# A channel-mixing MLP and an S4D convolution on one core: the 64-row remainder of layer 1 as three matmuls in two row halves of the array

## The chip, the core and the metric

The kernel runs on one core of a Trainium2 chip. The metric is device time in microseconds (us) of one execution; the time before is 1094.99 us, the median of three runs (1094.75 to 1095.13). Six names recur. PE is TensorE (its weight loads are listed as PEld), DVE is VectorE, ACT is ScalarE, POOL is GpSimd, and SP is the engine that issues most of the DMA transfers. PSUM is the memory into which PE writes, in banks of 512 float32 per partition.

## The reference

For 2048 tokens of 576 channels the kernel computes a normalisation, two branches from it, and their gated product with a skip connection:

```python
xn = _layernorm(x)
s = _A_ref(xn, ...)              # S4D: a convolution over all 2048 tokens, one kernel K per channel,
                                 #   K = 2 Re sum_n C[d,n] exp(A[d,n] dt[d] l), plus u * D_skip
g = _silu(_B_ref(xn, ...))       # MLP: layernorm -> 576x4608 (+b1) -> gelu -> 4608x576 (+b2)
return x + s * g
```

All values are float32, so the kernel has to keep more digits than one reduced-precision pass of PE gives.

## The kernel before

**The MLP** is most of PE's work. Its operands are split into a high part (rounded to float32r, a reduced form of float32) and a low part (what the rounding lost), and three products are summed in PSUM: high by high, high by low, low by high. The 4608 hidden features are cut into 12 groups of three tiles of 128 (`G = 3`), and the 2048 tokens into four blocks of 512. A *slot* is one group with one block: 48 slots, numbered from 0. Two blocks share a sweep over all groups, so the slots run in two sweeps of 24. A slot has eleven *positions*: three of layer 1 (one for each hidden tile, `layer1`) and eight of layer 2 (`layer2`, 72 matmuls of 288 columns).

**Layer 1** of a tile multiplies 576 input channels, which are four blocks of 128 rows and a remainder of 64. The four blocks take 12 matmuls with 512 columns (`w1h` with `XH`, `w1h` with `XL`, `w1l` with `XH`). The remainder takes two more. `XR` holds its 64 high rows above its 64 low rows, `w1r` holds the high weights twice, and `w1s` (called `r2` in the code) holds the low weights twice; `w1r` by `XR` and `w1s` by `XR` are full matmuls of 128 rows. So a tile has 14 matmuls, of which the last is needed for 64 rows only.

**The 64-row form.** `pair` (L608) computes that last product another way, ahead of the tile: with 64 rows of weights, in one half of the array's rows. For tile 0 it uses the upper half with `XR[:64]`, for tile 2 the lower half with a copy of the same rows in partitions 64 to 127 (`XQ`, loaded by `load_pair`, L604; it borrows the memory of `bias2` and is called `bias` in the profile). The two write two halves of one PSUM tile (`Q1[0]`), and `BEGUN` tells `layer1` to leave out the full matmul and not to clear PSUM. Tile 1 keeps its full one. The copy is loaded in 42 of the 48 slots, during the slot before; not where `bias2` is in use.

**The S4D branch** is computed as short *visits* of PE between the MLP's matmuls: `kgen` (L1042 in the profile) makes the convolution's kernel; `x1` (L1157), `k1` (L1188) and `s2` (L1217) are forward transform steps, `inv` (L1260) and `i1` (L1286) inverse ones. All of them split the array into smaller tiles of rows and columns; `x1` alone uses the shape that `pair` uses, 64 rows by 128 columns. DVE and ACT work between the visits.

**The order** of all engines' work is written out when the program is built. The class `Order` keeps a clock for each engine, charges each step an estimated duration, and puts steps into the program in that order. Dense work (layers 1 and 2) goes through `unit`; after a position `pe_turns` looks through lines of waiting steps (`c1`, `c3`, `kl` for S4D) and inserts visits whose inputs should be there, subject to spacing rules (`END`, `EDGE`, `ALONE`, `DUE`). With `edge`, at the end of a slot, it puts `pair` ahead of the visit, if the weights and the copy should have arrived; without a visit there, the slot has no pair. `hold` and the table `HOLD` delay single steps by hand. The names `mxa` and `mxb` are two PSUM tiles of two banks each that slots take in turn (`mx`); `cv` names those of the visits.

Of the kernel before, what the change touches and what calls it, by code (L numbers as in the profile page):

```python
# [18 lines left out]
P = 128  # L19
# [13 lines left out]
G = 3  # L33
NG = F // (P * G)
KB = 4
TB = 512
# [15 lines left out]
class Order:  # L52
# [44 lines left out]
    def take(self, eng, dur, ready, tbl=None):  # L97
        start = max(self.t[eng], ready)
        if eng == "DVE" and self.shared and start < self.t["POOL"] - 0.4:
            dur *= 1.1  # L100
        if tbl and tbl != self.tbl:
            dur += 1.28
            self.tbl = tbl
        self.t[eng] = start + dur
        return start + dur + self.LAT
# [119 lines left out]
def mixer_kernel(ctx, tc, u, log_a_real, a_imag, c_real, c_imag, log_dt, d_skip, w1, b1, w2, b2,  # L225
                 f1, f2, g2, g1, tvals, ident, out, parts=("mlp", "s4d")):
    nc = tc.nc
# [6 lines left out]
    def bank2(name):  # L234
        return ps.tile([P, 2, TB], F32, name=name, bufs=2 if name == "cv" else 1)
# [134 lines left out]
    acc = sb.tile([P, 8, D], F32, name="acc")  # L370
# [30 lines left out]
    MV, SECOND, PAIR, M4, SINGLE = {}, [], {}, [], {}  # L401
# [70 lines left out]
    XR = sb.tile([P, 2, TB], F32R, name="XR")  # L472
    XQ = {}
# [58 lines left out]
    W = {}  # L532
# [56 lines left out]
    HID, LAST, Q1, Q2, IDM = {}, {}, {}, {}, []  # L589
    turn = [0]  # L590

    def mx(i):
        return "mxa" if (turn[0] + i) % 2 == 0 else "mxb"

    BEGUN = set()
# [10 lines left out]
            XQ[0] = sb.tile([P, D], F32R, name="bias2")[:, :TB]  # L606
        nc.sync.dma_start(XQ[0][64:].bitcast(F32), XR[:64, tb].bitcast(F32))

    def pair(tb):

        Q1[0] = bank2(mx(1))
        for e, x in enumerate((XR[:64, tb], XQ[0][64:])):
            r, k = slice(64 * e, 64 * e + 64), e * (G - 1)
            nc.tensor.matmul(Q1[0][:, e], W[1][3][r, k * P:(k + 1) * P], x, start=True, stop=False,  # L616
                             skip_group_check=True)
        BEGUN.update((0, G - 1))

    def layer1(g, tb, i):  # L620
        h, lo, r1, r2 = W[1]
        c = slice(i * P, (i + 1) * P)
        if i < 2 and i not in BEGUN:
            Q1[i] = bank2(mx(i))
        q = Q1[i % 2][:, i // 2]
        ops = []
        for a, b in ((h, XH), (h, XL), (lo, XH)):
            ops += [(a[:, kb, c], b[:, kb, tb]) for kb in range(KB)]
        ops.append((r1[:, c], XR[:, tb]))
        if i not in BEGUN:  # L630
            ops.append((r2[:, c], XR[:, tb]))
        for j, (a, b) in enumerate(ops):
            nc.tensor.matmul(q, a, b, start=j == 0 and i not in BEGUN, stop=j == len(ops) - 1, skip_group_check=True)  # L633
        return hidden(g, tb, i, q)

    def first_layer1(i):


        h, lo, r1, r2 = W[1]
        if i != 1:  # L640
            Q1[i] = bank2("mxb" if i else "mxa")
        q = Q1[2][:, 0] if i == 2 else Q1[0][:, i]
        pairs = [(h, XH, 0), (h, XH, 1), (h, XL, 0), (h, XH, 2), (h, XL, 1), (h, XH, 3), (h, XL, 2), (h, XL, 3)]

        if i != 1:
            for j, (a, b, kb) in enumerate(pairs):
                for k in ((0, 1), (2,))[i // 2]:
                    nc.tensor.matmul(Q1[k // 2 * 2][:, k % 2], a[:, kb, k * P:(k + 1) * P], b[:, kb, 0],  # L648
                                     start=j == 0, stop=False)
        c = slice(i * P, (i + 1) * P)  # L650
        for kb in range(KB):
            nc.tensor.matmul(q, lo[:, kb, c], XH[:, kb, 0], start=False, stop=False)
        for r in (r1, r2):
            nc.tensor.matmul(q, r[:, c], XR[:, 0], start=False, stop=r is r2)

        return [hidden(0, 0, k, Q1[k // 2 * 2][:, k % 2]) for k in ((), (0, 1), (2,))[i]]
# [296 lines left out]
    def tables(b):  # L953
# [37 lines left out]
        def weigh(part):  # L991
# [10 lines left out]
            else:  # L1002
# [7 lines left out]
                 step("DVE", dve(SB * NV), f(phase, 0), need=[("kg", b - 2)] if b > 1 else []),  # L1010
                 step("DVE", dve(n), f(phase, 1), hold=HOLD.get(("phase", b), 0)), step("ACT", act(SB * NV), whole),
                 step("DVE", dve(SB * NV), frac, hold=HOLD.get(("frac", b), 0)), step("ACT", act(SB * NV), fold, mark=("fold", b))],
                [step("ACT", act(SB * NV), f(sin, 0), need=[("fold", b)], mark=("sin", b, 0), tbl="sin"),
# [55 lines left out]
        return behind  # L1069


    X1, S2, INV, I1, KG = 1.5, 1.75, 2.15, 3.05, 1.03

    HOLD = {("weigh", 19, 3): 1, ("phase", 19): 1, ("frac", 18): 2, ("k", 2, 1): (2, 1), (2, 0, 24): 1, (2, 1, 24): 1, ("k1", 2, 1, 2): 1}

    def chunk(c):

# [240 lines left out]
    NPOS = G + 8  # L1318
    NSLOT = 4 * NG
    od = Order(tc, nc)  # L1320
    od.pinned = True
    el, wl2, wl, nl2, pl, pl2, nl, ml, ml2, xl, wx, c3, c2, c1, c4, kl, tl, sl, vl, gl, odl, fl = [od.line() for _ in range(22)]
    nlh, mlh, mlt = od.line(), od.line(), od.line()
    od.lines = od.lines[-3:] + od.lines[:-3]

# [76 lines left out]


    L1 = 14 * 0.2315
    LEN = [L1] * G + [3 * n * 0.132 + 0.02 for n in (4, 2, 2, 4, 3, 3, 3, 3)]

    T0 = 12.5
    for e, t in dict(PE=0.0, ACT=4.6, DVE=3.7, POOL=3.8, SP=0.0).items():
# [71 lines left out]
    def weigh_in(which):  # L1480

        m = KB + 1 if which == 1 else G
        end = od.t["PE"] + sum(LEN[G:] if which == 1 else LEN[:G])
        for i in range(m):
# [22 lines left out]
    def wmark(n, which):  # L1507

        per = KB + 1 + G
        a = n * per + (0 if which == 1 else KB + 1)  # L1510
        return [("w", k) for k in range(a, a + (KB + 1 if which == 1 else G))]
# [23 lines left out]
    for k in range(8):  # L1535
        gl["steps"].append(step("POOL", 0.7, lambda k=k: part.update({k: load_f2(k)}), mark=("f2", k),
                                need=[("f2c", k - 2)] if k > 1 else ["turns"]))
        fl["steps"].append(step(None, 4.5, lambda: None, need=[("f2", k)]))
        for f in range(2):
            fl["steps"].append(step("ACT", act(256), lambda k=k, f=f: part[k](f), mark=("f2c", k) if f else None,  # L1540
                                    need=[("f2s", k - 1)] if k and k % 2 == 0 else []))
# [33 lines left out]


    pace = dict(left=NCH * (2 + 2 + 4), last=0.0, started=False)
    END = 1000.0


    EDGE = 0.2, 0.6
    ALONE, DUE = 20.0, (160.0, 950.0)

    def pe_turns(limit=1, any_time=False, all_lines=True, edge=None):
        for x in (nl, pl, ml) + ((c3, c1, kl) if all_lines else ()):
            n = 0
            while n < (2 if x in (c1, nl) else limit):
                h = od.head(x)
                if h is None or h[0]["eng"] != "PE" or h[1] > od.t["PE"] + (0.3 if x is nl else -0.4):
                    break  # L1590
                if x is c1:
                    now = od.t["PE"]
                    gap = (END - now) / max(pace["left"], 1)
                    if n == 0 and pace["started"] and now < pace["last"] + EDGE[edge is None] * gap and not any_time:
                        break
                    pace["started"], pace["last"] = True, now
                    pace["left"] -= 1
                if x is kl and pace["started"]:
                    b = kl["steps"][0]["mark"][1]
                    wait = ("wu", b + 1) not in od.marks or od.t["PE"] < DUE[0] + b * (DUE[1] - DUE[0]) / NB  # L1600
                    if b < NB - 1 and od.t["PE"] < h[1] + (ALONE if wait else 3.0):
                        break
                if edge is not None and not BEGUN and x in (c3, c1, kl):
                    m = wmark(edge // 2, 1) + [("xq", edge)]
                    if all(k in od.marks and od.marks[k] < od.t["PE"] - 0.3 for k in m):
                        od.unit(lambda: pair(edge % 2), 0.24)
                behind = ride(h[0]) if x in (c1, c3) else None
                od.run(x)
                if behind:
                    behind()  # L1610
                od.pin()
                od.advance(od.t["PE"])
                n += 1

    LATER = {}

    def later(slot, pos, f):
# [22 lines left out]

        return od.t["PE"] + sum(LEN[k % NPOS] for k in range(pos + 1, q))

    GAP = 0.17

    def hidden_by(pos, i, o=0):
        n = when(pos, o + (G if i < G - 1 else G + 2))
# [24 lines left out]
    for slot in range(NSLOT):  # L1671
        turn[0] = slot + 1
        od.shared = slot > 1
        g, tb = slot // 2 % NG, slot % 2
        n = slot // 2
        final = slot >= NSLOT - 2
        for pos in range(NPOS):
            if pos < G:
                need = wmark(n, 1) + [("x", tb)]
                if pos == 0:  # L1680
                    od.force(lambda: all(m in od.marks for m in need))

                    if slot in (1, 2 * NG + 1):
                        od.marks["x", tb] -= 2.3
                cell = []
                od.unit(lambda: cell.extend([layer1(g, tb, pos)] if slot else first_layer1(pos)),
                        L1 * (14 - (pos in BEGUN)) / 14 if slot else L1 * (22, 6, 14)[pos] / 14, need)
                if pos == 2:
                    BEGUN.clear()
                    k = slot % (2 * NG)  # L1690
# [16 lines left out]
            else:  # L1707
                j, terms, last, hid = l2_terms(pos - G)
                need = [wmark(n, 2)[i] for i in hid] + [("h", slot, i) for i in hid]
# [6 lines left out]
                cell = []  # L1716
# [3 lines left out]
                b = 8 + 4 * tb + j  # L1720
                if halves:
                    dh = terms[0][1]
                    od.marks["z", dh] = od.t["PE"] + od.LAT
                    x = od.line()
# [3 lines left out]
                if split:  # L1728
                    add = cell[0]
                    for d in range(2) if j == 0 else (terms[0][1],):  # L1730
                        m = ("acc", slot, j, d)
# [3 lines left out]
                        x = od.line()  # L1735
# [3 lines left out]
                if last and not halves:  # L1739
# [4 lines left out]
                    elif final:  # L1744
                        x = el if slot < NSLOT - 1 else od.line()
# [12 lines left out]
            for f in LATER.get((slot, pos), ()):  # L1758
                f()
            od.advance(od.t["PE"])  # L1760
            pe_turns(edge=slot + 1 if pos == NPOS - 1 else None, all_lines=pos in (0, 1, 2, G + 1, G + 3, G + 5, NPOS - 1))
    od.force(lambda: not od.urgent and not any(x["steps"] for x in od.lines))


# [52 lines left out]
```

## Time and profile before

| What | Value |
|---|---|
| Median of three runs | 1094.99 us (1094.75 to 1095.13) |
| The profiled execution, its own time | 1095.67 us |
| Its span, first to last instruction | 1093.9 us |
| Granted TensorE clock, mean | 0.999 |
| PE busy, DVE busy, ACT busy | 99%, 82%, 66% of the span |
| Matmuls of 64 rows by `pair`, L616 | 32, in 16 slots |
| Loads of the copy, `bias<-XR` | 42 |

In rows of the profile a group reads: line, engine, operation, what is written and read, shape, and how often; then busy time and mean duration. A row of the timeline reads: start in us, length in us, engine, line, operation, names, shape of the array's tile (rows\*columns), operand, and how many instructions follow each other under that name. A matmul's length is its latency; successive matmuls overlap, so what one costs PE is the distance to the next start. The visits' float32 matmuls are run as two instructions each, so `kgen` has 64 in the profile and 32 in the program's order.

### The profile page before, as it was taken

How to read it: one execution, taken by the hardware profiler on the slowest of the kernel's cores; microseconds unless marked ns; L12 is line 12 of the kernel's file. 1: busy time of each engine (PE TensorE's matmuls, PEld its weight loads, DVE VectorE, ACT ScalarE, POOL GpSimd, SP SyncE). 2: the span in 40 equal slices, each digit the busy share in tenths (PEclk: the TensorE clock that was granted, in tenths of full speed). 3: DMA queues.
4: the chain of work that ended last, by engine and by line, in shares of the span. 5: the costliest groups of instructions: out<-in, count | busy, mean ns of one | idle time of the engine just before them, and what ended most of it. 6: DMA issues, size and time to landing. Idle time of an engine off the chain costs nothing.

```text
span 1093.9 us, 27052 instructions
## 1 busy us (share of the span) xinstructions
PE 1087.1 (99%) x11445; PEld 954.0 (87%) x11445; DVE 891.9 (82%) x1302; ACT 727.1 (66%) x1113; POOL 188.4 (17%) x261
## 2 busy tenths in 40 slices
PE   9999999999999999999999999999999999999998
PEld 7989899899888898888988888888888888888897
DVE  7798667889998879889899987997969888766367
ACT  6585699778676674767767848685675757534333
POOL 4566210153020100001100000000001021101132
PEclk9999999999999999999999999999999999999999
DMA  8746764626354152355624215143142434454444
GB/s 242 225 149 152 236 235 143 179 80 157 116 160 134 44 112 67 96 110 148 161 48 118 78 56 141 34 122 87 56 126 42 144 101 132 114 170 150 137 151 103
DMA packets 139553, 138.22 MB, mean 126 GB/s; under 512 B 88952, under 2 KB 105016, under 8 KB 138856
## 3 DMA queue, kind: packets, MB, share of 16 engines
q1 hardware_dynamic: 124424, 85.05, 29.0%
q0 software_dynamic: 14528, 50.71, 14.7%
q8 instruction: 89, 1.46, 0.6%
q10 hardware_dynamic: 480, 0.74, 0.3%
q14 instruction: 32, 0.26, 0.1%
HBM read 102.17 MB, written 36.63 MB: 127 GB/s over the span
## 4 chain that ended last, share of the span: by engine, by line
PE 95%; DVE 3%; ACT 1%; SPq 1%; issue 0%; DMA 0%; POOL 0%; DVEq 0%; ACTq 0%; POOLq 0%
PE mxb L707 20%; PE mxa L707 20%; PE mxa L633 20%; PE mxb L633 20%; PE cv L1217 3%; PE cv L1042 3%; PE cv L1260 2%; PE cv L1286 2%; PE cv L1188 1%; PE cv L1157 1%; PE mxa L1348 1%; DVE acc L717 0%; PE mxa L648 0%; SPq L1089 0%; PE mxb L616 0%
## 5 line engine op out<-in xcount | busy, mean ns | idle before, releaser
L677 DVE TENSOR_TENSOR hl<-h,hh 128x512 fp32r<-128x512 f32 x144 | 98.5, 687 | 99.2 <-ACT hh L674 98.4
L707 PE MATMUL mxa<-w2h,hh 128*128 128x288 f32 x573 | 170.3, 297 | 0.0
L707 PE MATMUL mxb<-w2h,hh 128*128 128x288 f32 x573 | 170.2, 297 | 0.0
L707 PE MATMUL mxb<-w2h,hl 128*128 128x288 f32 x573 | 169.3, 295 | 0.1
L707 PE MATMUL mxa<-w2h,hl 128*128 128x288 f32 x573 | 169.1, 295 | 0.0
L707 PE MATMUL mxa<-w2l,hh 128*128 128x288 f32 x573 | 168.6, 294 | 0.0
L707 PE MATMUL mxb<-w2l,hh 128*128 128x288 f32 x573 | 168.6, 294 | 0.0
L671 ACT ACTIVATE h<-mxa,b1t 128x512 f32<-128x512 f32 x73 | 50.1, 687 | 98.3 <-PE mxa L633 95.1
L707 PEld LDWEIGHTS mxa<-w2h,hh 128*128 128x128 f32 x573 | 107.6, 188 | 5.8 <-issue 3.0
L707 PEld LDWEIGHTS mxb<-w2h,hh 128*128 128x128 f32 x573 | 107.6, 188 | 4.3 <-issue 1.4
L707 PEld LDWEIGHTS mxb<-w2l,hh 128*128 128x128 f32 x573 | 107.6, 188 | 0.8
L707 PEld LDWEIGHTS mxa<-w2l,hh 128*128 128x128 f32 x573 | 107.6, 188 | 0.6
L707 PEld LDWEIGHTS mxb<-w2h,hl 128*128 128x128 f32 x573 | 107.5, 188 | 0.3 <-DVE hl L677 0.3
L707 PEld LDWEIGHTS mxa<-w2h,hl 128*128 128x128 f32 x573 | 107.5, 188 | 0.0
L671 ACT ACTIVATE h<-mxb,b1t 128x512 f32<-128x512 f32 x71 | 48.8, 687 | 69.7 <-PE mxb L633 67.2
L674 ACT ACTIVATE hh<-h 128x512 fp32r<-128x512 f32 x144 | 90.7, 631 | 3.7
L944 POOL DMA_DIRECT2D par<-par_s x36 | 27.8, 771 | 367.8 <-DVE mg L988 325.0
L717 DVE TENSOR_TENSOR acc<-mxa,acc 128x576 f32<-128x576 f32 x87 | 65.5, 753 | 26.0 <-PE mxa L707 25.9
L717 DVE TENSOR_TENSOR acc<-mxb,acc 128x576 f32<-128x576 f32 (+1 forms) x89 | 65.9, 741 | 17.8 <-PE mxb L707 17.7
L633 PE MATMUL mxa<-XH,w1h 128*128 128x512 f32 x284 | 79.2, 401 | 0.0
L633 PE MATMUL mxb<-XH,w1h 128*128 128x512 f32 x280 | 77.7, 399 | 0.0
L633 PE MATMUL mxa<-XL,w1h 128*128 128x512 f32 x284 | 76.1, 390 | 0.0
(277 smaller groups left out, 2494.4 us busy)
## 6 DMA issues: line engine op xcount, KB each, us to landing
raw<-in_B_w_dram SPq DMA_DIRECT2D x72, 288.0 KB, 3.4
raw<-in_B_w_dram SPq DMA_DIRECT2D x96, 192.0 KB, 3.5
par_s<-A POOLq DMA_DIRECT2D x4, 2160.0 KB, 8.1
par<-par_s POOLq DMA_DIRECT2D x36, 240.0 KB, 3.6
f2t<-f2q SPq DMA_DIRECT2D x24, 256.0 KB, 3.6
g2t<-g2p SPq DMA_DIRECT2D x24, 256.0 KB, 4.1
bias<-XR SPq DMA_DIRECT2D x42, 128.0 KB, 3.6
raw<-in_B_w_dram SPq DMA_DIRECT2D x48, 96.0 KB, 3.7
```

Of the source, the lines that this page charges most:

```text
L633: nc.tensor.matmul(q, a, b, start=j == 0 and i not in BEGUN, stop=j == len(ops) - 1, skip_group_check=True)
L671: nc.scalar.activation(t, q, AF.Gelu_apprx_tanh, bias=b1t[:, k:k + 1], scale=1.0)
L674: LAST[0] = nc.scalar.activation(hh[:, i], t, AF.Copy)
L677: nc.vector.tensor_sub(hl[:, i], t, hh[:, i].bitcast(F32))
L707: nc.tensor.matmul(q[:, dh, :288], a[:, i, c], b[:, i, d], start=i == 0 and k == 0 and alone != 1, stop=i == G - 1 and k == 2, skip_group_ ...
L717: nc.vector.tensor_add(o, q[:, dh:dh + n, :288], b)
L944: nc.gpsimd.dma_start(PAR[b].rearrange("p (g i) k -> p g (i k)", g=4), dram(par_s, (b // 3 * 48 + b % 3 * 4) * NPAR, [[D * NPAR, P], [12 * ...
L1042: nc.tensor.matmul(q[32 * g:32 * g + 32, i // 2, i % 2 * 64:i % 2 * 64 + 64], U[:, ri, 4 * g + i, :], v[:, ri, 4 * g + i, :], start=ri == ...
L1157: nc.tensor.matmul(Q[24 * v][:, e], FP[0][r, f, 0], x[r, 12 * e:12 * e + 12], start=n == 0, stop=n == 2, skip_group_check=True)
L1217: nc.tensor.matmul(Q[i][32 * q:32 * q + 32, f, ri::2], m[r, 4 * i + q, 32 * ri:32 * ri + 32], A2[r, 4 * p + 2 * i + q // 2, :, :, q % 2], ...
L1260: nc.tensor.matmul(QI[q // 2][64 * f:64 * f + 64, q % 2, i], MAT["g2t", p + i // 2][r, i % 2, f, ri], YS[p + i // 2][0][r, i % 2, ri, f], ...
L1286: nc.tensor.matmul(Q[h][64 * y:64 * y + 64, t], g1t.rearrange("p a e -> p (a e)"), A2[:, k:k + 2, 1].rearrange("p i d r -> p i r d"), star ...
```

## The change

`pair` now issues three matmuls, for all tiles of a slot: tile 0 in the upper row half, tile 2 in the lower, tile 1 in the upper half again, into a second PSUM tile (`Q1[1]`). They come at one of two places. At the edge of a slot they stand *behind* the visits, if there were any, and if the addition of the slot before that reads the second PSUM tile should be done. Otherwise they stand *within* layer 1, after tile 0 (`late`), behind visits that are put there or, where there are none, by themselves; tile 0's sum then ends with them. Numbers of the planner change too: charged durations of the visits, `END`, `EDGE`, `ALONE`, `DUE`, the order of two lines, and the table `HOLD` is emptied. Layer 2, the visits' own matmuls and all loads are as before.

```diff
-    def pair(tb):
-        Q1[0] = bank2(mx(1))
-        for e, x in enumerate((XR[:64, tb], XQ[0][64:])):
-            r, k = slice(64 * e, 64 * e + 64), e * (G - 1)
-            nc.tensor.matmul(Q1[0][:, e], W[1][3][r, k * P:(k + 1) * P], x, start=True, stop=False,
-                             skip_group_check=True)
-        BEGUN.update((0, G - 1))
+    def pair(tb, late):
+        r2, x = W[1][3], (XR[:64, tb], XQ[0][64:])
+        def mm(e, q, i, a, n, start=True, stop=False):
+            nc.tensor.matmul(q[:, a:a + n], r2[64 * e:64 * e + 64, i * P:(i + 1) * P], x[e][:, a:a + n], start=start,
+                             stop=stop, skip_group_check=True)
+        if not late:
+            Q1[0] = bank2(mx(1))
+        Q1[1] = bank2(mx(1 if late else 2))
+        mm(0, Q1[0][:, 0], 0, 0, TB, not late, late)
+        mm(1, Q1[0][:, 1], 2, 0, TB)
+        mm(0, Q1[1][:, 0], 1, 0, TB)
+        BEGUN.update(range(G))
...
-    X1, S2, INV, I1, KG = 1.5, 1.75, 2.15, 3.05, 1.03
-    HOLD = {("weigh", 19, 3): 1, ("phase", 19): 1, ("frac", 18): 2, ("k", 2, 1): (2, 1), (2, 0, 24): 1, (2, 1, 24): 1, ("k1", 2, 1, 2): 1}
+    X1, S2, INV, I1, KG = 1.38, 1.69, 1.99, 3.19, 1.03
+    HOLD = {}
...
-    END = 1000.0
-    EDGE = 0.2, 0.6
-    ALONE, DUE = 20.0, (160.0, 950.0)
+    END = 974.0
+    EDGE = 0.34, 0.29
+    ALONE, DUE = 18.4, (108.0, 794.0)
+    PAIR = 0.62, 0.53
...
-                if edge is not None and not BEGUN and x in (c3, c1, kl):
-                    m = wmark(edge // 2, 1) + [("xq", edge)]
-                    if all(k in od.marks and od.marks[k] < od.t["PE"] - 0.3 for k in m):
-                        od.unit(lambda: pair(edge % 2), 0.24)
+                away += x in (c3, c1, kl)
...
+        if away and edge is not None and not BEGUN:
+            m = wmark(edge // 2, 1) + [("xq", edge), ("acc", edge - 1, 3)]
+            if all(k in od.marks and od.marks[k] < od.t["PE"] - 0.2 for k in m):
+                od.unit(lambda: pair(edge % 2, False), PAIR[1])
+        return away
...
+                late = pos == 0 and slot and not BEGUN and od.marks.get(("xq", slot), 1e9) < od.t["PE"] + 2.5
...
+                if late:
+                    od.advance(od.t["PE"])
+                    away = pe_turns(all_lines=LATE_TOO)
+                    od.unit(lambda: pair(tb, True), PAIR[away > 0])
```

What the change moves on PE is seen at three places. The first is slot 3, in which no visit is due yet. PE's order from the end of layer 1's tile 0, before:

```order
L633 MATMUL mxa<-XH,w1l 128x512 x4
L633 MATMUL mxa<-XR,w1r 128x512
L633 MATMUL mxa<-XR,w1s 128x512
L633 MATMUL mxb<-XH,w1h 128x512 x4
L633 MATMUL mxb<-XL,w1h 128x512 x4
L633 MATMUL mxb<-XH,w1l 128x512 x4
L633 MATMUL mxb<-XR,w1r 128x512
L633 MATMUL mxb<-XR,w1s 128x512
```

and of the change:

```order
L639 MATMUL mxa<-XH,w1l 128x512 x4
L639 MATMUL mxa<-XR,w1r 128x512
L616 MATMUL mxa<-XR,w1s 128x512
L616 MATMUL mxa<-bias_773,w1s 128x512
L616 MATMUL mxb<-XR,w1s 128x512
L639 MATMUL mxb<-XH,w1h 128x512 x4
L639 MATMUL mxb<-XL,w1h 128x512 x4
L639 MATMUL mxb<-XH,w1l 128x512 x4
L639 MATMUL mxb<-XR,w1r 128x512
```

The full matmul with `w1s` is gone from each tile, and the three of L616 stand alone between full matmuls. Counted over the whole order, this form is in 18 slots.

The second place is the slot's edge ahead of the first `x1`. PE's order there, before (L707 is layer 2, L1157 the visit):

```order
L707 MATMUL mxa<-w2h,hl 128x288
L616 MATMUL mxb<-XR,w1s 128x512
L616 MATMUL mxb<-bias_773,w1s 128x512
L1157 MATMUL cv<-pr,f2t 128x384 x4
L1157 MATMUL cv<-ys,f2t 128x384 x4
L1157 MATMUL cv<-pr,f2t 128x384 x4
L633 MATMUL mxb<-XH,w1h 128x512 x4
```

and of the change, where L714 is layer 2 and L1164 the visit:

```order
L714 MATMUL mxa<-w2h,hl 128x288
L1164 MATMUL cv<-pr,f2t 128x384 x4
L1164 MATMUL cv<-ys,f2t 128x384 x4
L1164 MATMUL cv<-pr,f2t 128x384 x4
L616 MATMUL mxb<-XR,w1s 128x512
L616 MATMUL mxb<-bias_773,w1s 128x512
L616 MATMUL mxa<-XR,w1s 128x512
L639 MATMUL mxb<-XH,w1h 128x512 x4
```

Two matmuls ahead of the visit have become three behind it. Counted over the whole order, 24 slots have the three behind a visit, 11 of them at an edge like this one and 13 within layer 1; in two of the 24 the visit just ahead is `x1`.

The third place is a visit within layer 1: slot 8, whose `kgen` (L1042, in the change L1049) stood after tile 1. Before:

```order
L633 MATMUL mxb<-XR,w1r 128x512
L633 MATMUL mxb<-XR,w1s 128x512
L633 MATMUL mxa<-XH,w1h 128x512 x4
L633 MATMUL mxa<-XL,w1h 128x512 x4
L633 MATMUL mxa<-XH,w1l 128x512 x4
L633 MATMUL mxa<-XR,w1r 128x512
L633 MATMUL mxa<-XR,w1s 128x512
L1042 MATMUL cv<-w 32x64 x32
```

and of the change:

```order
L639 MATMUL mxb<-XR,w1r 128x512
L1049 MATMUL cv<-w 32x64 x32
L616 MATMUL mxb<-XR,w1s 128x512
L616 MATMUL mxb<-bias_773,w1s 128x512
L616 MATMUL mxa<-XR,w1s 128x512
L639 MATMUL mxa<-XH,w1h 128x512 x4
L639 MATMUL mxa<-XL,w1h 128x512 x4
L639 MATMUL mxa<-XH,w1l 128x512 x4
```

The visit has moved one tile earlier and carries the three 64-row matmuls behind it.

More of the change, by code (lines that the diff above doesn't have):

```diff
@@ L99, in take @@
         if eng == "DVE" and self.shared and start < self.t["POOL"] - 0.4:
-            dur *= 1.1
+            dur *= 1.13
         if tbl and tbl != self.tbl:
@@ L607, in load_pair, with layer1 @@
         nc.sync.dma_start(XQ[0][64:].bitcast(F32), XR[:64, tb].bitcast(F32))
-    def pair(tb):
-        Q1[0] = bank2(mx(1))
-        for e, x in enumerate((XR[:64, tb], XQ[0][64:])):
-            r, k = slice(64 * e, 64 * e + 64), e * (G - 1)
-            nc.tensor.matmul(Q1[0][:, e], W[1][3][r, k * P:(k + 1) * P], x, start=True, stop=False,
-                             skip_group_check=True)
-        BEGUN.update((0, G - 1))
-    def layer1(g, tb, i):
+    def pair(tb, late):
[10 more added lines that the diff above has]
+        BEGUN.update(range(G))
+    def layer1(g, tb, i, late=False):
         h, lo, r1, r2 = W[1]
@@ L629, in layer1 @@
         ops.append((r1[:, c], XR[:, tb]))
-        if i not in BEGUN:
+        if i not in BEGUN and not late:
             ops.append((r2[:, c], XR[:, tb]))
         for j, (a, b) in enumerate(ops):
-            nc.tensor.matmul(q, a, b, start=j == 0 and i not in BEGUN, stop=j == len(ops) - 1, skip_group_check=True)
+            nc.tensor.matmul(q, a, b, start=j == 0 and i not in BEGUN, stop=j == len(ops) - 1 and not late,
+                             skip_group_check=True)
         return hidden(g, tb, i, q)
@@ L1321, in mixer_kernel @@
     od.pinned = True
-    el, wl2, wl, nl2, pl, pl2, nl, ml, ml2, xl, wx, c3, c2, c1, c4, kl, tl, sl, vl, gl, odl, fl = [od.line() for _ in range(22)]
+    el, wl2, wl, nl2, pl, pl2, nl, ml, ml2, xl, wx, c3, c2, kl, c1, c4, sl, tl, vl, gl, odl, fl = [od.line() for _ in range(22)]
     nlh, mlh, mlt = od.line(), od.line(), od.line()
@@ L1404, in mixer_kernel @@
     L1 = 14 * 0.2315
-    LEN = [L1] * G + [3 * n * 0.132 + 0.02 for n in (4, 2, 2, 4, 3, 3, 3, 3)]
+    LEN = [L1] * G + [3 * n * 0.1318 + 0.02 for n in (4, 2, 2, 4, 3, 3, 3, 3)]
     T0 = 12.5
@@ L1577, in mixer_kernel @@
     pace = dict(left=NCH * (2 + 2 + 4), last=0.0, started=False)
-    END = 1000.0
-    EDGE = 0.2, 0.6
-    ALONE, DUE = 20.0, (160.0, 950.0)
+    END = 974.0
+    EDGE = 0.34, 0.29
+    ALONE, DUE = 18.4, (108.0, 794.0)
+    PAIR = 0.62, 0.53
     def pe_turns(limit=1, any_time=False, all_lines=True, edge=None):
+        away = 0
         for x in (nl, pl, ml) + ((c3, c1, kl) if all_lines else ()):
@@ L1588, in pe_turns @@
                 h = od.head(x)
-                if h is None or h[0]["eng"] != "PE" or h[1] > od.t["PE"] + (0.3 if x is nl else -0.4):
+                if h is None or h[0]["eng"] != "PE" or h[1] > od.t["PE"] + (0.3 if x is nl else -0.23):
                     break
@@ L1613, in pe_turns @@
                 n += 1
+        if away and edge is not None and not BEGUN:
[3 more added lines that the diff above has]
+        return away
+    TURNS, LATE_TOO = (1, 2, G + 1, G + 3, G + 5, NPOS - 1,), True
     LATER = {}
@@ L1641, in when @@
         return od.t["PE"] + sum(LEN[k % NPOS] for k in range(pos + 1, q))
-    GAP = 0.17
+    GAP = 0.18
     def hidden_by(pos, i, o=0):
@@ L1685, in mixer_kernel @@
                 cell = []
-                od.unit(lambda: cell.extend([layer1(g, tb, pos)] if slot else first_layer1(pos)),
-                        L1 * (14 - (pos in BEGUN)) / 14 if slot else L1 * (22, 6, 14)[pos] / 14, need)
+                late = pos == 0 and slot and not BEGUN and od.marks.get(("xq", slot), 1e9) < od.t["PE"] + 2.5
+                od.unit(lambda: cell.extend([layer1(g, tb, pos, late)] if slot else first_layer1(pos)),
+                        L1 * (14 - (pos in BEGUN or late)) / 14 if slot else L1 * (22, 6, 14)[pos] / 14, need)
+                if late:
+                    od.advance(od.t["PE"])
+                    away = pe_turns(all_lines=LATE_TOO)
+                    od.unit(lambda: pair(tb, True), PAIR[away > 0])
                 if pos == 2:
@@ L1760, in mixer_kernel @@
             od.advance(od.t["PE"])
-            pe_turns(edge=slot + 1 if pos == NPOS - 1 else None, all_lines=pos in (0, 1, 2, G + 1, G + 3, G + 5, NPOS - 1))
+            if pos or not late:
+                pe_turns(edge=slot + 1 if pos == NPOS - 1 else None, all_lines=pos in TURNS)
     od.force(lambda: not od.urgent and not any(x["steps"] for x in od.lines))
```

## Prediction

> **What bounds the kernel now.** I read the page's busy times and its chain of work first, then PE's waits, and then single stretches of PE's timeline.
>
> ```profile
> PE 1087.1 (99%) x11445; PEld 954.0 (87%) x11445; DVE 891.9 (82%) x1302; ACT 727.1 (66%) x1113; POOL 188.4 (17%) x261
> PE 95%; DVE 3%; ACT 1%; SPq 1%; issue 0%; DMA 0%; POOL 0%; DVEq 0%; ACTq 0%; POOLq 0%
> ```
>
> PE is busy throughout and is 95% of the chain that ended last. A busy PE need not be at its peak, so the next question is whether it ever waits for another engine. This is the whole answer of the view of waits for PE:
>
> ```profile
> PE mxa L1348 <- POOL XL L1341: 1.3, 1, 1.3
> PE mxa L648 <- ACT XH L520: 0.4, 1, 0.4
> ```
>
> Both are at the start, 1.7 us together. So the time is a sum of distances between starts on PE, and a change is worth what it does to that sum; other engines matter only if they begin to hold PE up. How the sum is made shows where a visit interrupts dense work. PE's timeline around a lone `kgen` (L1042):
>
> ```profile
> 172.89 1.07 PE L633 MATMUL mxa<-XH,w1l 128*128 128x512 f32 x4
> 173.80 0.39 PE L633 MATMUL mxa<-XR,w1r 128*128 128x512 f32 x1
> 174.02 0.39 PE L633 MATMUL mxa<-XR,w1s 128*128 128x512 f32 x1
> 174.34 1.10 PE L1042 MATMUL cv<-w 128*32 128x64 f32 x64
> 175.38 1.20 PE L633 MATMUL mxb<-XH,w1h 128*128 128x512 f32 x4
> 176.41 1.08 PE L633 MATMUL mxb<-XL,w1h 128*128 128x512 f32 x4
> ```
>
> Three prices are here. A dense matmul of 512 columns costs (173.80 - 172.89) / 4 = 0.2275 us. **Going in** costs: from the last dense start to the visit's are 174.34 - 174.02 = 0.32, so 0.09 more than a dense step. **Coming out** costs: the first four dense starts take 176.41 - 175.38 = 1.03 where four take 0.91, about 0.11 more. The array's shape changes at both ends (128\*128, 128\*32, 128\*128).
>
> **What the full 64-row form costs today.** The groups of the low weights `w1s`:
>
> ```profile
> L633 PE MATMUL mxa<-XR,w1s x57: 388/389/389, 37.1 to 1078.4; 128*128 128x512 f32 x57
> L633 PE MATMUL mxb<-XR,w1s x52: 388/388/391, 40.3 to 1075.2; 128*128 128x512 f32 x52
> L616 PE MATMUL mxb<-XR,w1s x9: 498/498/498, 250.4 to 958.4; 64*128 64x512 f32 x9
> L616 PE MATMUL mxa<-XR,w1s x7: 498/498/498, 319.9 to 933.1; 64*128 64x512 f32 x7
> ```
>
> A full one has a latency of 389 ns, the first one of `pair` 498 in all 16 cases. The 109 ns are its weight load, which nothing covers after a change of shape; it is also the 0.11 seen on coming out. Two cases of `pair`, ahead of `inv` (L1260) and ahead of `x1` (L1157):
>
> ```profile
> 319.70 0.29 PE L707 MATMUL mxb<-w2h,hl 128*128 128x288 f32 x1
> 319.92 0.50 PE L616 MATMUL mxa<-XR,w1s 64*128 64x512 f32 x1
> 319.92 0.50 PE L616 MATMUL mxa<-bias,w1s 64*128 64x512 f32 x1
> 320.35 1.83 PE L1260 MATMUL cv<-ys,g2t 32*64 32x96 f32 x128
> 322.11 1.20 PE L633 MATMUL mxa<-XH,w1h 128*128 128x512 f32 x4
> ...
> 250.22 0.29 PE L707 MATMUL mxa<-w2h,hl 128*128 128x288 f32 x1
> 250.44 0.50 PE L616 MATMUL mxb<-XR,w1s 64*128 64x512 f32 x1
> 250.44 0.50 PE L616 MATMUL mxb<-bias,w1s 64*128 64x512 f32 x1
> 250.78 0.52 PE L1157 MATMUL cv<-pr,f2t 64*128 64x384 f32 x4
> 251.13 0.51 PE L1157 MATMUL cv<-ys,f2t 64*128 64x384 f32 x4
> 251.48 0.51 PE L1157 MATMUL cv<-pr,f2t 64*128 64x384 f32 x4
> 251.93 1.20 PE L633 MATMUL mxb<-XH,w1h 128*128 128x512 f32 x4
> ```
>
> The two halves do run at once: both start in the same 10 ns. Yet ahead of `inv` they cost 320.35 - 319.92 = 0.43, and the two dense matmuls that they replace 2 x 0.2275 = 0.455; a gain of 0.025. Ahead of `x1`, whose shape is the same, they cost 0.34, and `x1` is shorter too: 251.93 - 250.78 = 1.15. Alone it takes 1.25:
>
> ```profile
> 540.63 0.39 PE L633 MATMUL mxb<-XR,w1s 128*128 128x512 f32 x1
> 540.95 0.62 PE L1157 MATMUL cv<-pr,f2t 64*128 64x384 f32 x4
> 541.41 0.51 PE L1157 MATMUL cv<-ys,f2t 64*128 64x384 f32 x4
> 541.76 0.51 PE L1157 MATMUL cv<-pr,f2t 64*128 64x384 f32 x4
> 542.20 0.40 PE L707 MATMUL mxa<-w2h,hh 128*128 128x288 f32 x1
> ```
>
> So there `pair` costs 0.34 - 0.10 = 0.24 net. Of the 16 old pairs five stand ahead of `x1` and eleven ahead of another visit: together 5 x 0.24 + 11 x 0.43 = 5.93 us.
>
> **The price of three.** The trace has no third matmul in a half. Its start follows the first one's by the uncovered load and one stream, 0.109 + 0.2275 = 0.337; the row from `pair` to `x1`, 250.44 to 250.78, is just that step, the same half twice. From the last start to what follows in another shape it takes 0.43 - 0.109 = 0.32. Together 0.657. From below, the third would cost nothing beyond the two, 0.43; from above, its weights would not load under the first one's stream, 0.657 + 0.109 = 0.766. `x1` is the nearest row: from 541.41 to 541.76 are two steps of two halves, 0.175 each for 384 columns, while its first two steps, 540.95 to 541.41, take 0.46, 0.11 more. The uncovered load is paid once at the visit's start and not again. I take 0.657.
>
> Three dense matmuls are 0.6825. **Behind a visit** the three gain 0.025, because the visit's change of shape is there anyway. **By themselves** they pay going in and coming out as well, 0.09 + 0.109 = 0.199: they cost 0.856 and lose 0.174. Behind `x1` they need no change of shape and no uncovered load: 0.657 - 0.199 = 0.458.
>
> **The sum.** Counted in the order: 94 full matmuls fewer (15 of the 109 are left); 40 units of three at 0.657 and two behind `x1` at 0.458; the 16 old pairs gone; and the places where dense work goes over into split shapes are 93, before 74. Of the 19 more, 18 are the lone threes and one comes of the visits' new places.
>
> - full matmuls: -94 x 0.2275 = -21.39
> - old pairs: -5.93
> - new threes: 40 x 0.657 + 2 x 0.458 = +27.20
> - going in and out: 19 x 0.199 = +3.78
>
> This is +3.7 us: the 24 behind a visit gain about 1.0, the 18 alone lose 3.1, the old pairs' gain of 1.3 is given up, and one more interruption costs 0.2. The steps are read to 10 ns; over 42 slots that leaves some 0.4 us either way. The profiled execution's own 1095.67 (its span of 1093.9 and 1.8 around it) is 0.68 over the median; from the median, 1094.99 + 3.7 = 1098.7 us.
>
> [...]
>
> **What is costed at nothing.** The 42 copies are loaded as before, on SP's queue during the slot before. Tile 0's gelu on ACT now waits for the late three, and behind a late visit for that too, at most an `i1`. Behind it on ACT queue its rounding copy and tile 1's gelu, and DVE's `hl` waits for these. The cover is tiles 1 and 2, 26 x 0.2275 = 5.9 us on PE, before layer 2 needs tile 0. The edge form needs the second PSUM tile, which DVE's last addition of the old slot reads, a layer-1 tile earlier; the visit in between covers it, and if DVE is late, PE waits up to one addition (0.75) in at most 11 slots. Layer 2's wait on DVE is the thin spot:
>
> ```profile
> L707 PEld LDWEIGHTS mxb<-w2h,hl 128*128 128x128 f32 x573 | 107.5, 188 | 0.3 <-DVE hl L677 0.3
> L717 DVE TENSOR_TENSOR acc<-mxb,acc 128x576 f32<-128x576 f32 (+1 forms) x89 | 65.9, 741 | 17.8 <-PE mxb L707 17.7
> ```
>
> It has cost 0.3 us in the whole run, with steps held back by hand. That table is emptied and the visits are elsewhere, so new waits of some tenths each are likelier than fewer, as there is nothing to remove. I put 0 into the sum and leave room above.
>
> **The rivals.**
>
> *New waits on PE* (0.11). The planner's changed numbers let DVE work collide with `hl` or with the additions: eight collisions of 0.2 to 0.5 us would add 1.6 to 4, giving 1100.3 to 1102.7. For it: DVE is 82% busy and the hand-made delays are gone. Against it: 1.7 us of waits before, both outside the slots.
>
> *The third's weights are not covered* (0.04). 42 x 0.109 = 4.6 more: 1103.3. The steps of `x1` speak against it. [...]
>
> *The pair's changes of shape are cheaper than the rows say* (faster, 0.06). If the load of 0.109 were covered at the start of the 40 threes and after the 18 lone ones, the sum would lose 58 x 0.109 = 6.3: -2.7 us, 1092.3. The planner's own charges (0.53 behind a visit, 0.62 alone) amount to this. It decides once the units cost 0.09 us less each, on the average of 42. Against it: 498 ns without exception in 16 pairs, and the longer first group after each visit.
>
> *Somewhat cheaper threes* (no change, 0.07): threes some 0.04 to 0.14 cheaper than 0.657, from a cause that these rows don't show, and the sum shrinks to within 0.2%.
>
> That fewer slots would have the new form is ruled out, as the order holds 42.
>
> **How the numbers follow.** The forecast, +3.7 with its 0.4 and up to 1.5 of waits, has 0.72. A measurement of this kernel can tell about 0.2%, 2.2 us, from no change; forecast, waits and uncovered third are slower by more than that: 0.87. No change has 0.07, faster 0.06. The range reaches from 1096.8, inside the case of no change, to 1101.4, into the new waits; beyond lie most of the faster case, the uncovered third and heavy waits.
>
> **What would show it.** In the changed profile: `w1s` groups of 15 full and 126 of L616; first and second of three at 498 ns and the third near 389; around a lone three starts at 0.32, 0.34 and 0.32, and then a first dense group 0.11 longer; around a `kgen` three no second going-in. PE's waits stay below 3 us. A third with 498 ns or a step of 0.45 shows the uncovered load; PE waits for DVE `hl` or `acc` show the new waits. If lone threes cost under 0.68, or the time is below 1096, the pricing of the changes of shape is wrong.

## The result

The changed kernel takes 1100.97 us (median of six runs, 1099.94 to 1101.62) where the kernel before takes 1095.06 in the same runs: a ratio of 1.0053, 95% interval 1.0040 to 1.0066. In a later batch it took 1100.23 against 1095.28, 1.0047 (1.0034 to 1.0059). It is slower, by 5.9 and 4.95 us; the forecast was 3.7.

The page of the changed kernel, busy times and chain:

```profile
span 1098.8 us, 27069 instructions
PE 1091.0 (99%) x11445; PEld 943.3 (86%) x11445; DVE 891.3 (81%) x1302; ACT 723.5 (66%) x1110; POOL 187.5 (17%) x261
PE 98%; DVE 1%; DMA 0%; ACT 0%; issue 0%; SPq 0%; ACTq 0%
```

PE still sets the time. This is the whole view of its waits:

```profile
PE mxa L1355 <- POOL XL L1348: 1.3, 1, 1.3
PE cv L516 <- DVE row L456: 0.5, 1, 0.5
PE mxa L655 <- ACT XH L520: 0.4, 1, 0.4
PE cv L1267 <- issue: 0.3, 1, 0.3
```

The first three are in the head of the program. The second is not in the profile of the kernel before, but the layer-1 matmul that comes next starts at 12.7 us in both. No slot shows a wait for DVE or ACT in this view. The fourth, inside an inverse visit and ended by no semaphore, is new; it comes back below. The groups of `w1s`, four of the 64-row matmuls and two of the full ones:

```profile
L616 PE MATMUL mxa<-XR,w1s x42: 383/444/501, 75.8 to 1076.6; 64*128 64x512 f32 x42
L616 PE MATMUL mxb<-XR,w1s x42: 385/393/503, 76.1 to 1077.0; 64*128 64x512 f32 x42
L616 PE MATMUL mxa<-bias,w1s x22: 393/499/502, 75.8 to 1076.6; 64*128 64x512 f32 x22
L616 PE MATMUL mxb<-bias,w1s x20: 384/501/502, 95.1 to 1057.4; 64*128 64x512 f32 x20
L639 PE MATMUL mxb<-XR,w1s x8: 388/388/389, 40.6 to 593.9; 128*128 128x512 f32 x8
L639 PE MATMUL mxa<-XR,w1s x7: 388/389/389, 37.4 to 590.8; 128*128 128x512 f32 x7
```

There are 126 of L616 and 15 full ones. The `XR` groups mix first and third matmuls, so their latencies lie near both 390 and 500. PE's timeline shows the two apart. First three by themselves in slot 3:

```profile
75.50 0.39 PE L639 MATMUL mxa<-XR,w1r 128*128 128x512 f32 x1
75.81 0.49 PE L616 MATMUL mxa<-XR,w1s 64*128 64x512 f32 x1
75.82 0.50 PE L616 MATMUL mxa<-bias,w1s 64*128 64x512 f32 x1
76.15 0.39 PE L616 MATMUL mxb<-XR,w1s 64*128 64x512 f32 x1
76.47 1.20 PE L639 MATMUL mxb<-XH,w1h 128*128 128x512 f32 x4
77.50 1.07 PE L639 MATMUL mxb<-XL,w1h 128*128 128x512 f32 x4
```

The starts are 0.31, 0.34 and 0.32 us apart, the third has a latency of 0.39, and the first dense group after takes 1.03 instead of 0.91. Taken to the nanosecond, all 18 lone threes last 657 or 658 ns from their first start to the next dense one. The same behind `x1`, at the second place of the change:

```profile
253.05 0.52 PE L1164 MATMUL cv<-pr,f2t 64*128 64x384 f32 x4
253.39 0.39 PE L616 MATMUL mxb<-XR,w1s 64*128 64x512 f32 x1
253.41 0.38 PE L616 MATMUL mxb<-bias,w1s 64*128 64x512 f32 x1
253.62 0.39 PE L616 MATMUL mxa<-XR,w1s 64*128 64x512 f32 x1
253.95 1.19 PE L639 MATMUL mxb<-XH,w1h 128*128 128x512 f32 x4
```

Here no weight load is uncovered (0.39 each), and the three take 0.56.

### The profile page after: what moved, and what is told of

Same layout as the page of the kernel before. It is cut to its first block, busy times and chain, and to the rows that moved or that the text cites. A ratio compares the mean times of both kernels' runs of the same rounds, so it can differ in the third digit from the quotient of the medians.

```text
span 1098.8 us, 27069 instructions
## 1 busy us (share of the span) xinstructions
PE 1091.0 (99%) x11445; PEld 943.3 (86%) x11445; DVE 891.3 (81%) x1302; ACT 723.5 (66%) x1110; POOL 187.5 (17%) x261
## 4 chain that ended last, share of the span: by engine, by line
PE 98%; DVE 1%; DMA 0%; ACT 0%; issue 0%; SPq 0%; ACTq 0%
PE mxb L714 21%; PE mxa L714 21%; PE mxa L639 20%; PE mxb L639 20%; PE cv L1049 3%; PE cv L1224 3%; PE cv L1267 2%; PE cv L1293 2%; PE cv L1195 1%; PE cv L1164 1%; PE mxa L616 1%; PE mxb L616 1%; DMA acc<-in_A_u_dram 0%; PE mxa L655 0%; PE cv L516 0%; DVE A L816 0%
## 5 line engine op out<-in xcount | busy, mean ns | idle before, releaser
L714 PE MATMUL mxa<-w2h,hh 128*128 128x288 f32 x573 | 170.6, 298 | 0.0
L714 PE MATMUL mxb<-w2h,hh 128*128 128x288 f32 x573 | 170.3, 297 | 0.0
L714 PE MATMUL mxa<-w2h,hl 128*128 128x288 f32 x573 | 169.3, 295 | 0.0
L714 PE MATMUL mxb<-w2h,hl 128*128 128x288 f32 x573 | 169.0, 295 | 0.0
L714 PE MATMUL mxb<-w2l,hh 128*128 128x288 f32 x573 | 168.7, 294 | 0.0
L714 PE MATMUL mxa<-w2l,hh 128*128 128x288 f32 x573 | 168.6, 294 | 0.0
L714 PEld LDWEIGHTS mxa<-w2h,hh 128*128 128x128 f32 x573 | 107.6, 188 | 5.6 <-issue 3.5
L714 PEld LDWEIGHTS mxb<-w2h,hh 128*128 128x128 f32 x573 | 107.6, 188 | 5.4 <-issue 2.2
L714 PEld LDWEIGHTS mxb<-w2l,hh 128*128 128x128 f32 x573 | 107.6, 188 | 0.7
L714 PEld LDWEIGHTS mxa<-w2l,hh 128*128 128x128 f32 x573 | 107.6, 188 | 0.6
L714 PEld LDWEIGHTS mxa<-w2h,hl 128*128 128x128 f32 x573 | 107.5, 188 | 0.3 <-DVE hl L684 0.2
L714 PEld LDWEIGHTS mxb<-w2h,hl 128*128 128x128 f32 x573 | 107.5, 188 | 0.0
```

The costliest lines, as they stand in the source:

```text
L714: nc.tensor.matmul(q[:, dh, :288], a[:, i, c], b[:, i, d], start=i == 0 and k == 0 and alone != 1, stop=i == G - 1 and k == 2, skip_group_ ...
```

## The experiments

Two theories stand against each other. **A**: the loss is the changes of the array's shape, priced by rows. **B**: it is the moved order and the emptied table of delays. Each run is compared with the kernel before in its own batch: 1095.65 for the first four rows of the table, 1095.28 for the last four, which are the later batch named above. The changed kernel itself did not run in the batch of the first four, so there its distance is taken as 5.9 or 4.95 us.

| Run | Median us | Ratio to before, 95% interval |
|---|---|---|
| e1_lone_full | 1097.36 | 1.0014 (1.0005 to 1.0022) |
| e2_all_full | 1097.88 | 1.0020 (1.0011 to 1.0029) |
| e3_two | 1099.83 | 1.0034 (1.0022 to 1.0046) |
| b0_before_full | 1097.10 | 1.0010 (1.0002 to 1.0019) |
| after_again | 1100.23 | 1.0047 (1.0034 to 1.0059) |
| b_nohold | 1097.06 | 1.0016 (1.0007 to 1.0024) |
| b_new | 1102.79 | 1.0069 (1.0056 to 1.0081) |
| a_old_noh | 1111.32 | 1.0144 (1.0129 to 1.0160) |

### The lone threes undone

`full` issues tile 0's full matmul, and tiles 1 and 2 get theirs at their ends again; the planner is charged as before, so nothing else moves.

```diff
-                    od.unit(lambda: pair(tb, True), PAIR[away > 0])
+                    od.unit(lambda: (pair if away else full)(tb, True), PAIR[away > 0])
```

> The changed kernel with one edit: in the 18 slots where the three stood by themselves, the three low products are full matmuls of 128 rows again; all other instructions keep their places. Theory A (changes of the array's shape): each lone three costs 0.856 us and three full ones 0.68, so 18 x 0.174 = 3.1 us less than the changed kernel's 1100.97: about 1097.9. Theory B (the moved order and the emptied table of delays bring the loss, the 64-row form is nearly free): within 0.5 us of 1100.97. PE should go in and out of split shapes 75 times instead of 93.

It is 1.7 us over the kernel before, where the changed kernel is 4.95 to 5.9 over it: 3.2 to 4.2 us gone. PE's timeline at the same place in slot 3:

```profile
75.20 0.39 PE L647 MATMUL mxa<-XR,w1r 128*128 128x512 f32 x1
75.43 0.39 PE L630 MATMUL mxa<-XR,w1s 128*128 128x512 f32 x1
75.66 1.07 PE L647 MATMUL mxb<-XH,w1h 128*128 128x512 f32 x4
76.56 1.07 PE L647 MATMUL mxb<-XL,w1h 128*128 128x512 f32 x4
```

The starts are 0.23 apart, and no longer group follows. PE's last matmul starts at 1089.86 in this profile and at 1093.23 and 1092.79 in the two profiles of the changed kernel: 3.4 and 2.9 us earlier. So theory A's 3.1 us holds, and B's "within 0.5" doesn't.

### All threes undone

```diff
-                od.unit(lambda: pair(edge % 2, False), PAIR[1])
+                od.unit(lambda: full(edge % 2, False), PAIR[1])
...
-                    od.unit(lambda: pair(tb, True), PAIR[away > 0])
+                    od.unit(lambda: full(tb, True), PAIR[away > 0])
```

> The changed kernel with no 64-row matmul at all: all 42 slots have three full ones, all other instructions keep their places. Theory A: the 18 lone ones save 3.1 us, the 24 behind a visit give up 1.0: 1100.97 - 2.1 = 1098.9, 1.0 above the run without lone ones. Its distance to the kernel before without pairs should be 0.2 us if the order's other moves cost only the one interruption more, and 2 to 2.5 us if the moved order costs what the prediction's sum left out. Theory B: about 1101.

It takes 0.5 us more than the run above; 1.0 was expected, and the intervals of the two overlap. In the profiles PE's last matmul starts 1.0 us later (1090.85 against 1089.86). So the 24 threes behind a visit earn little, as priced. Against the old order without pairs, next, it is 0.8 us longer, between the two values set down; 0.35 us of that is, in the profile, a pause in the eleventh inverse visit, which comes back below.

### The old pairs undone

In the kernel before, the 16 pairs are charged but not issued:

```diff
-                        od.unit(lambda: pair(edge % 2), 0.24)
+                        od.take("PE", 0.24, 0.0); BEGUN.update((0, G - 1)); FULL.update((0, G - 1))
```

> The kernel before with its 16 pairs replaced by full matmuls at the same places. Theory A: the pairs gained 5 x 0.215 beside x1 and 11 x 0.025 elsewhere, 1.35 us: 1096.4. If a pair gains what the planner charges for it (0.24 for two full ones of 0.46), 16 x 0.22 = 3.5 us: 1098.6.

It is 1.45 us over the kernel before; the rows gave 1.35, the planner's charges 3.5. That gain was small, and the change gave it up.

### Two matmuls in place of three

```diff
-        Q1[1] = bank2(mx(1 if late else 2))
...
-        mm(0, Q1[1][:, 0], 1, 0, TB)
+        FULL.add(1)
```

> The changed kernel with two matmuls in the halves (tiles 0 and 2) in all 42 slots, and tile 1's low product as a full matmul again, at the same places. Theory A: the third in a half takes a whole stream, 0.2275 us, as the full one does, so nothing changes: 1101.0 within 0.5. If the third rides along for less, this run is slower than the changed kernel, by up to 42 x 0.2275 = 9.6 us; if it is dearer, faster.

It is 4.2 us over the kernel before, against 4.95 to 5.9 with three. The intervals overlap; it is not slower, so the third does not ride along for less. It is 0.75 to 1.7 us faster where at most 0.5 was expected: in the profiles PE's last matmul starts 0.5 and 1.0 us earlier (1092.26), of which a shorter pause in the eleventh inverse visit is 0.1 to 0.2, and the rest is not placed. PE's timeline in slot 3:

```profile
75.06 0.39 PE L639 MATMUL mxa<-XR,w1r 128*128 128x512 f32 x1
75.38 0.50 PE L616 MATMUL mxa<-XR,w1s 64*128 64x512 f32 x1
75.39 0.50 PE L616 MATMUL mxa<-bias,w1s 64*128 64x512 f32 x1
75.82 1.18 PE L639 MATMUL mxb<-XH,w1h 128*128 128x512 f32 x4
```

Two take 0.44 and a full one 0.2275, together what three take, 0.66. The third matmul, with nothing beside it in the other half, costs a whole stream, as the full one does.

### The changed kernel again

The changed kernel without an edit, in the later batch.

> The changed kernel itself once more, beside the runs of the same batch. Its PE rows add up to 3.7 us over the kernel before, and its profile holds two pauses on PE of 0.4 and 0.6 us at single places. Theory A: if these are accidents of one execution, they are gone or elsewhere here, and the distance to the kernel before is 4 to 5 us. Theory B (the new order makes PE wait at fixed places): they are at the same places again and the distance stays near 5.9 us.

The distance is 4.95 us. The last matmul of the program in each profile gives PE's part of it. In the kernel before:

```profile
1088.56 0.29 PE L707 MATMUL cv<-w2h,hl 128*128 128x288 f32 x1
```

and in the changed one, later batch:

```profile
1092.79 0.29 PE L714 MATMUL cv<-w2h,hl 128*128 128x288 f32 x1
```

PE ends 4.23 us later; counted from the first layer-1 matmul of the head, 12.73 and 12.67, it is 4.29. Of the two pauses that the expectation names one is gone, four steps of 0.1 at 22.5 to 23.5 us that the first profile had. The other is at its old place:

```profile
980.76 1.76 PE L1267 MATMUL cv<-ys,g2t 32*64 32x96 f32 x121
982.82 0.39 PE L1267 MATMUL cv<-ys,g2t 32*64 32x96 f32 x7 [0.30 <-issue]
983.14 0.40 PE L714 MATMUL mxa<-w2h,hh 128*128 128x288 f32 x1
```

This visit takes 983.14 - 980.76 = 2.38, the other eleven 1.76: 0.62 us. With it the sum closes: 3.7 + 0.6 = 4.3 of 4.29. So the distance is the one that theory A gave, 4 to 5 us, while one of the two pauses is tied to its place, as B had it.

### The pause moved along the stream

```diff
-    warm_up(9)
+    warm_up(41)
```

> The changed kernel with 32 more warm-up matmuls in the head of the program, which compute nothing that is used; every later PE instruction stands 64 places further in its stream. The five profiles of programs with the changed order show a pause of PE of 0.3 to 0.6 us near the end of the eleventh inverse visit, with no semaphore that ends it. Theory P (supply of instructions: the pause belongs to a place in the stream): the eleventh inverse visit takes 1.76 us like the others, and a pause of 0.2 us or more may stand in another visit. Theory Q (it belongs to the work at that place): it takes 2.1 us or more again. The whole is longer by the warm-up that is not hidden, so only the visit is read.

> The same with 64 more warm-up matmuls, 128 places. Theory P: the eleventh inverse visit takes 1.76 us. Theory Q: 2.1 us or more.

One run of each was made (1107.32 and 1114.20 us, the kernel before 1096.45), and only the visits are read. The eleventh inverse visit with 64 more instructions ahead:

```profile
988.45 1.83 PE L1267 MATMUL cv<-ys,g2t 32*64 32x96 f32 x128
990.21 0.40 PE L714 MATMUL mxa<-w2h,hh 128*128 128x288 f32 x1
```

It is back at 1.76, and in the same profile another visit has a pause, the fifteenth `s2`:

```profile
723.91 0.91 PE L1224 MATMUL cv<-A,f2t 64*32 64x192 f32 x29
725.16 1.23 PE L1224 MATMUL cv<-A,f2t 64*32 64x192 f32 x35 [0.34 <-issue]
726.32 0.40 PE L714 MATMUL mxb<-w2h,hh 128*128 128x288 f32 x1
```

It takes 2.41 instead of 1.54. With 128 more, no visit has one. So theory Q is out: the pause does not belong to the work of that visit. A place in the instruction stream, theory P, fits, but the instructions put ahead also moved the visit in time (988.45 and 995.32 against 980.76), and no run separates the two.

The DMA packets in the traces speak for P. In all six profiles with such a pause PE goes on 2.2 to 2.4 us after a packet of 16384 bytes of the instruction queue (q8) started; in the changed kernel's first profile the packet starts at 980.98 and PE goes on at 983.22. The inverse visit at 622.17 of that profile has a packet at 621.91 and no pause (it takes 1.76), so a packet alone does not make one. What holds PE there was not tried.

### The emptied table alone

```diff
-    HOLD = {("weigh", 19, 3): 1, ("phase", 19): 1, ("frac", 18): 2, ("k", 2, 1): (2, 1), (2, 0, 24): 1, (2, 1, 24): 1, ("k1", 2, 1, 2): 1}
+    HOLD = {}
```

> The kernel before with the table of delays emptied and nothing else; PE's order is the same, 48 rows of DVE's and 9 of ACT's order differ. Theory A: no difference, within 0.3 us of the kernel before. Theory B: the delays kept DVE out of the way of layer 2, and without them PE waits 0.5 to 2 us, seen as waits of PE's weight loads for hl or acc.

It costs the kernel before 1.8 us, within the 0.5 to 2 that theory B had. Of PE's waits these are new:

```profile
PE cv L516 <- DVE row L456: 1.0, 1, 1.0
PE mxb L707 <- DVE hl L677: 0.5, 1, 0.5
PE mxa L707 <- ACT h L671: 0.3, 1, 0.3
```

The first is in the head of the program, ahead of anything the table delays; `b0_before_full`, which has the table, shows it too, with 1.4. The other two are at 567 to 570 us, and with what each adds in uncovered loads PE loses 1.3 us there, where the kernel before loses 0.35. This 1.0 and 0.3 from the head make up most of the 1.36 us by which PE's last matmul is later (1089.92 against 1088.56); the rest of the 1.8 is not placed. DVE's timeline just there shows what stood ahead of `hl`:

```profile
567.31 0.69 DVE L966 TENSOR_TENSOR w<-w,par 128x512 f32<-128x512 f32 x1
567.92 0.95 DVE L1136 TENSOR_TENSOR ys<-kt,pr 128x768 fp32r<-128x768 f32 x1
568.79 0.69 DVE L677 TENSOR_TENSOR hl<-h,hh 128x512 fp32r<-128x512 f32 x1
```

Two steps of the S4D branch, 1.5 us, came just ahead of the one that PE waited for. In the kernel before, `hl` came ahead of both:

```profile
567.50 0.69 DVE L677 TENSOR_TENSOR hl<-h,hh 128x512 fp32r<-128x512 f32 x1
568.10 0.69 DVE L966 TENSOR_TENSOR w<-w,par 128x512 f32<-128x512 f32 x1
568.70 0.96 DVE L1136 TENSOR_TENSOR ys<-kt,pr 128x768 fp32r<-128x768 f32 x1
```

In the changed kernel the table is empty too, but its order shows no such wait.

### The numbers swapped

The changed code with the old numbers (and the emptied table), and the kernel before with the new ones:

```diff
-    END = 974.0
-    EDGE = 0.34, 0.29
-    ALONE, DUE = 18.4, (108.0, 794.0)
+    END = 1000.0
+    EDGE = 0.2, 0.6
+    ALONE, DUE = 20.0, (160.0, 950.0)
...
```

> The changed code with the planner's old numbers (charges, END, EDGE, ALONE, DUE, order of lines), still with the table of delays emptied, since its entries name steps of another order. 42 threes, 18 of them alone, 92 goings-in instead of 93. Theory A: 0.2 us below the changed kernel. Theory B: the new numbers cost about 1 us or more, so 1 to 2 us below it.

> The kernel before with the planner's new numbers and the emptied table, and the old form of the pair. Only 5 slots get a pair, 2 of them beside x1, and goings-in are 75. Theory A: 11 pairs fewer (3 beside x1) and one going-in more, 3 x 0.215 + 8 x 0.025 + 0.2 = 1.05 us over the kernel before. Theory B: 2 us or more over it.

The old numbers cost the changed code 11.1 us, where both theories had a gain, 0.2 by A and 1 to 2 by B. The new ones cost the kernel before 7.5, where A had 1.05; B's "2 us or more" came true. In the changed code with old numbers PE waits inside slots:

```profile
PE mxb L639 <- ACT h L678: 2.9, 2, 2.6
PE mxb L714 <- DVE hl L684: 1.8, 1, 1.8
PE mxa L714 <- DVE hl L684: 1.5, 1, 1.5
```

These are 6.2 us; a slow stretch after the longest, shown in the last section, adds some 1.7, and from the last matmul to the end it takes 4.4 us longer (1101.41 to 1111.4, in the changed kernel 1092.79 to 1098.4). That is 12.3 of the 13.0 us between the two profiled executions; the slower one was 1.8 over its median. In the kernel before with the new numbers PE's last matmul is 4.5 us later, and the stretch behind it takes 2.8 longer (1093.10 to 1101.2, before 1088.56 to 1093.9).

The table is empty in both runs, so they do not separate the numbers from the table, whose loss alone costs 1.8 us in the kernel before. What they show is that numbers and table suit the order that they were chosen with. That the new numbers cost nothing in their own kernel no run shows by itself, but there PE has none of these waits.

No run beat the kernel before.

## Why the prediction was right, and where it fell short

**The bound** was right: PE's order sets the time, and no slot of the changed kernel shows a wait for DVE or ACT.

**The price of three** was right to the nanosecond: 0.657 expected, 0.657 to 0.660 on average by place. The choice among the two ends was right too; the third starts 0.335 after the first one, with a latency of 0.39 where an uncovered first one has 0.50, so its weights loaded under the first one's stream. Behind `x1` 0.458 net was expected; the three take 0.554, and `x1`'s last step is 0.10 shorter than alone (0.34 instead of 0.44), 0.45.

**Going in and out**: 93 places, 19 more, and the first four dense starts after a lone three at 1.03, as priced. The lone threes are most of the loss: without them 3.2 to 4.2 us go, 3.1 expected. The old pairs' gain of 1.35 was measured as 1.45, the gain of the 24, expected as 1.0, as 0.5 by the medians and about 1.0 by the start of PE's last matmul.

**The sum** of 3.7 is too small against 5.9 and 4.95. The step that was mis-sized is the one on what is costed at nothing. In the later batch PE accounts for 4.23: the 3.7, and 0.6 for a pause in the eleventh inverse visit. The rest of 4.95 is outside PE's stretch: from the last matmul to the end 5.6 us instead of 5.3 (1088.56 to 1093.9), and some 0.4 by which medians and spans of the two kernels differ. In the result's own batch the profile adds four steps of 0.1 near 23 us, and the median's distance is a further 0.7 above the profiled execution's own, 1100.91 - 1095.67 = 5.2: the kernel before was profiled in a run 0.6 above its median, the changed one in a run at its median. That scatter was taken off as if both shared it. Why the two batches differ by 1 us stays open; their intervals overlap.

**Luck.** The forecast's own band, +3.7 with its 0.4 and up to 1.5 of waits, ends at 1100.6. The measured 1100.97 lies above it, in the room that the range had for new waits, and 0.4 below the range's end. New waits did not come; a pause and scatter filled that room. That the range held the time is in part luck; the prices of the steps are not.

**The rivals.** New waits on DVE did not come, though the thin spot is real: the emptied table costs 1.8 us in the old order. The added pause has another cause, which the prediction did not have. An uncovered third, cheaper changes of shape, and the middle case are out by the rows: the third at 0.39 us, the first near 0.50 wherever the shape had changed. The third has the first one's rows, and its load is covered all the same: in slot 3 PEld's row for it starts at 75.92, where the first one started at 75.81 and the third starts at 76.15.

## What to carry to other kernels

Matmuls of half the array's rows are worth their place by three numbers read from a trace: the distance of dense starts (here 0.2275 us), the step into another array shape (0.09) and the uncovered weight load after it, on both sides (0.11 each). In this kernel three of them, run by themselves between full matmuls, cost 0.86 us against 0.68; next to work of the same shape they gain 0.2, next to split work of another shape almost nothing (0.657 to 0.660 against 0.6825), and an odd one in a half costs as much as a full one (0.22 against 0.2275). A planner's charge for such a step has to be checked against the distance between starts, and its other numbers belong to one order: here old numbers in the new order, and new ones in the old, cost more than the form did.

## What the runs showed that I had not expected

PE pauses of 0.35 to 0.87 us moved when instructions were put ahead. One stood near the end of the eleventh inverse visit in all five profiles of the changed order as it is (0.35 to 0.72), went when 64 or 128 instructions were put ahead, and then stood in another visit in one of the two (0.87). Both visits in which it was seen issue many small matmuls, 128 of 96 columns and 64 of 192.

PE's clock fell after one long wait. In the changed code with old numbers, windows of 3.0, 3.7 and 3.4 us around the longest wait (us of the stretch, its length, busy times, then the granted clock, the DMA share and GB/s):

```profile
259.90:262.90 3.00, 0.51 (x3) 0.09 (x1) 1.56 (x2) 2.97 (x4) 0.00 (x0) 1.00 1.03 365
262.90:266.60 3.70, 3.59 (x9) 2.83 (x10) 1.82 (x3) 3.49 (x6) 0.00 (x0) 0.54 0.96 129
266.60:270.00 3.40, 3.40 (x24) 3.17 (x22) 1.26 (x4) 1.32 (x2) 0.00 (x0) 1.00 0.00 0
```

After PE had stood idle for 2.6 us the clock was 0.54 over the next 3.7, then 1.00 again. In the timeline the groups of four dense matmuls there start at 263.01, 264.77 and 266.48, some 1.75 us apart instead of 0.91, so this wait cost 1.7 us more than its own length. After the waits of 1.8 and 1.5 us in the same run the clock stayed at 1.00. Why it fell after this wait and not after the other two no run shows.
